# Every second quad's bf16 product and the softmax normalisation on GpSimd instead of VectorE

## The chip, the cores and the metric

The kernel runs on one core of a Trainium2 chip. The metric is the device time of one execution in microseconds (us), as the median of several runs. The engines of a core are TensorE (PE; PEld are its weight loads), VectorE (DVE), ScalarE (ACT), GpSimd (POOL) and the DMA queues, here issued from SyncE (SP).

## The reference, cut to what matters

A transformer block with adaptive layer norm: attention with 32 heads of width 20 over 2048 tokens, then a bilinear gated MLP without a nonlinearity.

```python
x = A_x                                        # (1, 2048, 640), bf16
mod = (silu(c) @ w_mod).reshape(1, 6, 1, -1)   # sa, ca, ga, sb, cb, gb
h = layernorm(x) * (1 + ca) + sa
q, k, v = split_heads(h @ wqkv)                # H = 32, Dh = 20
p = softmax(q @ k.T * Dh ** -0.5)              # 32 x 2048 x 2048 exponentials
x = x + ga * (merge_heads(p @ v) @ wo)
h = layernorm(x) * (1 + cb) + sb
x = x + gb * (((h @ w_gate) * (h @ w_up)) @ w_down)   # F = 1536
```

## The kernel before

**Tiling.** The queries are cut into five chunks (`CHUNKS`: 512, 512, 512, 256, 256 tokens). The heads form 8 sets of 4, one head in each 32-row stripe of TensorE. One chunk with one set of heads is an *item*; there are 40, taken in order. In an item the scores of 128 keys by 512 columns for one head are a *unit*.

**Exponentials in two ways.** Most units go to ScalarE: `fexp` (L1219) takes three or two PSUM banks at once, in turn from the sets 0 to 2 and 3 to 4, and writes the buffers `PP`. The others, four at a time (a *quad*, 93 in all, numbered by `qi`), get their exponential from integer arithmetic on VectorE:

- `fp1` (L1244), four times for each quad: one PSUM bank of scores plus a constant, as int16, to a slot of `DB` (two slots). The PSUM bank comes from `G`, banks 5 and 6, which the rounds of all projections and of the MLP use as well.
- `fm` (L1272): the low seven bits of `DB` become a bf16 mantissa factor in a slot of `DSS` (three slots).
- `fx` (L1277): the product of `DB`, read as bf16, with that slot, in place. It is the quad's first term, and it gives the `DB` slot back together with `fe`.
- `fe` (L1280): the exponent bits alone, into another slot of `DSS`: the quad's second term.

The PV matmuls (L1616) take ScalarE's `PP` and both terms of each quad, and add them up in PSUM bank 7, which holds one item at a time; column 0 of each head gathers the sum of the exponentials. When an item is complete, `item_end_tasks` (L1319) puts out four instructions in a chain: `t1` transposes bank 7 to `OT` (L1325), `t2` takes the reciprocals of the sums to `invT` (L1328), `t3` multiplies `OT` by them into `OTn` (L1330), and `t4` transposes this back to `OcT` (L1333), from where DMAs collect it in `Ocp` for the output projection. The chunk's MLP (`suffix`, L1366) is worked off while the next chunk's exponentials run; the last chunk's stands alone at the end. Its layer norm has two small steps on GpSimd, L1423 and L1425.

**The order is written by a planner.** `Sched` simulates the engines with a cost for each task, and takes for each engine at each moment the ready task of the lowest priority number; `emit_program` writes the orders found as five fixed instruction streams with semaphore waits. At run time each engine works through its own stream in that order, and an instruction that waits holds up all that stand behind it on its engine. The costs used for the parts concerned are `TS_4X, TT_2X = 600.0, 1145.0` (ns, for `fm`/`fe` and `fx`), 60 ns for a semaphore (`SEM`), and 60 ns of latency for a GpSimd task. The steps of a quad wait until bank 7 belongs to their item:

```python
t = Task("dve", dur, f, deps, prio=2.5 + .001 * qi, name=f"{name}.{qi}")
t.cond = lambda: it <= st_pv["item"]
```

How many quads an item has is a table (`QUADS`, L389), and the change leaves it as it is.

Of the kernel before, what the change touches and what calls it, by code (L numbers as in the profile page):

```python
# [6 lines left out]
ALU = mybir.AluOpType  # L7
# [58 lines left out]
class Slots:  # L66

    def __init__(self, ids, name=""):
        self.name = name
        self.free = [(i, []) for i in ids]  # L70
        self.hold = {}

    def avail(self, only=None):
# [9 lines left out]
        return best  # L83

    def take(self, k, refs=1):
        i, rel = self.free.pop(k)
        self.hold[i] = [refs, []]
        return i, rel

    def done(self, i, task):  # L90
        h = self.hold[i]
        h[0] -= 1
        h[1] = [x for x in h[1] if x.nbytes or x.eng != task.eng] + [task]
        if h[0] == 0:
            del self.hold[i]
            self.free.append((i, h[1]))

# [292 lines left out]
D_LEAD = 0.35  # L390
NB0, NSS = 2, 3
NPS = 4
TS_4X, TT_2X = 600.0, 1145.0
# [38 lines left out]
def build_kernel(nc, A_x, A_wqkv, A_wo, B_x, B_w_gate, B_w_up, B_w_down, c, w_mod, out):  # L432
    S, D, H, DH = A_x.shape[1], A_x.shape[2], 32, 20
    KD = D // 128
# [166 lines left out]

    G = Slots([5, 6], "G")
    GX = Slots([2, 3, 4], "GX")
    GC = Slots([0, 1], "GC")
# [142 lines left out]

    def quarters(n, lhs, rhs, st, sp):
        def one(x):
            return lambda e, b: e.matmul(ps[32 * x:32 * x + 32, b, 0:n], lhs()[:, 32 * x:32 * x + 32], rhs(),  # L750
                                         tile_position=(0, 32 * x), start=st, stop=sp, skip_group_check=True)
        return [one(x) for x in range(4)]
# [72 lines left out]
    def hT_rounds(tc, prio):  # L825
# [3 lines left out]
        for k in range(KD):  # L829
# [6 lines left out]
            def after(r, k=k):  # L836
# [6 lines left out]
            r = Round(mms, [t_xn[tc][i] for i in range(4)] + [p_id], after, prio, name=f"hT{tc}.{k}",  # L843
                      banks=GX if tc == 0 and k in (1, 3, 4) else None)
            t_hT[tc].append(r.evac[0])
# [212 lines left out]
    while ap < NA:  # L1058
        even = len(glist) % 2 == 0
        us = ubuf[ap:ap + (3 if even else 2)]  # L1060
        apos.append(ap)
        ap += len(us)
        glist.append((us, 0 if even else 3))
# [128 lines left out]
    act_tasks = []  # L1192
    gx_evac = [t_hT[0][k] for k in (1, 3, 4)]
    act_of = {}
# [56 lines left out]
    for qi, (it, us) in enumerate(dquads):  # L1251
# [30 lines left out]
        tm = term(fm, list(st_["p1"]), TS_4X, "M", slot=0)  # L1282
        term(fx, [tm], TT_2X, "X", src=0, last=True)
        term(fe, list(st_["p1"]), TS_4X, "EX", slot=1, src=1, last=True)
# [34 lines left out]
    def item_end_tasks(it):  # L1319
# [9 lines left out]
                                            OT[:, 0:n].rearrange("p (b c) -> p b c", c=32)[:, :, 0:1]), [t1], prio=1.5)  # L1329
        t3 = dve(sb_cost(n, 1.04), lambda e: e.tensor_tensor(  # L1330
            OTn[:, 0:n].rearrange("p (b c) -> p b c", c=32), OT[:, 0:n].rearrange("p (b c) -> p b c", c=32),
            invT[:, 0:nb32].unsqueeze(2).to_broadcast([128, nb32, 32]), ALU.mult), [t2], prio=1.5)
        t4 = dve(n * 1.1 + 65, lambda e: e.transpose(OcT[:, cell["s"], 0:n], OTn[:, 0:n]), [t3], prio=1.5)  # L1333
# [32 lines left out]
    def suffix(ci):  # L1366
# [88 lines left out]
        for fc in range(FT):  # L1455
            use_x = tail and fc < nsx
            wbuf, dm = [], []
            for w_, wv in enumerate((wgv, wuv)):
# [16 lines left out]
                dm.append(t)  # L1475
            gs = fc % 2
            for w_ in range(2):
                mms = []
# [202 lines left out]

    tail_added = [False]

    def d_wants():
# [78 lines left out]
    def pick_pe(t):  # L1763
        sc.pull("pe")
        g = pvstate["sidx"]
        if g < NG:
            ts, us = score_q[g]
            if acquire_ready(ts, t):
                start = mode_start("S", t)
# [33 lines left out]
        elif not tail_added[0]:  # L1803
            tail_added[0] = True
            la = [a for a in act_tasks[-2:]]
            if all(a.done is not None for a in la):
                for b in range(5):
                    G.add(b, la)
            else:
# [3 lines left out]
        if XFIRST and ring() >= XFIRST and pick_x(t):  # L1813
            just_s[0] = False
            return True
        cands = pv_candidates(t, PVCAP)
# [101 lines left out]
```

The softmax here doesn't subtract the row's maximum and nothing guards it: scores larger than these inputs give would overflow.

## Time and profile before

| | us |
|---|---|
| median of 3 runs (853.17 to 856.5) | 854.6 |
| the profiled execution | 851.11 |
| its span, from the first to the last instruction | 849.3 |
| busy: PE, DVE, ACT, POOL | 793.9, 719.6, 778.7, 30.6 |
| the 671 exponentials on ACT (L1220) | 763.0 |
| `fp1`, x372 | 250.4 |
| `fx`, x93 | 112.2 |
| `fm` and `fe`, x93 each | 63.3 each |
| `t3`, x40 | 23.1 |

Busy time counts an instruction from its start to its end, and two VectorE instructions in a row overlap by almost 0.1 us, so that VectorE's sum is a little above the time it was taken. The profile's groups give for each line of the kernel the engine, the tiles written and read, the count, the busy time and the mean of one, and the idle time ahead of them with the engine and line that ended it.

### The profile page before, as it was taken

How to read it: one execution, taken by the hardware profiler on the slowest of the kernel's cores; microseconds unless marked ns; L12 is line 12 of the kernel's file. 1: busy time of each engine (PE TensorE's matmuls, PEld its weight loads, DVE VectorE, ACT ScalarE, POOL GpSimd, SP SyncE). 2: the span in 40 equal slices, each digit the busy share in tenths (PEclk: the TensorE clock that was granted, in tenths of full speed). 3: DMA queues.
4: the chain of work that ended last, by engine and by line, in shares of the span. 5: the costliest groups of instructions: out<-in, count | busy, mean ns of one | idle time of the engine just before them, and what ended most of it. 6: DMA issues, size and time to landing. Idle time of an engine off the chain costs nothing.

```text
span 849.3 us, 28015 instructions
## 1 busy us (share of the span) xinstructions
PE 793.9 (93%) x12239; PEld 306.9 (36%) x12239; DVE 719.6 (85%) x1271; ACT 778.7 (92%) x700; POOL 30.6 (4%) x65
## 2 busy tenths in 40 slices
PE   8899999999998999999989999998999999999898
PEld 4432333322223222223323223232344443454477
DVE  7769988899999989898889999889789979677773
ACT  4568899999999999999999999999999999999931
POOL 2300000000001000000001000000011000000000
PEclk9989999999999999999999999999999999999999
DMA  9135222012240122310210122000300236115420
GB/s 296 37 97 158 61 68 58 7 44 76 75 124 18 33 60 57 109 57 13 68 40 6 24 65 56 14 12 14 70 33 6 59 76 135 38 46 113 105 59 20
DMA packets 114433, 53.19 MB, mean 63 GB/s; under 512 B 83359, under 2 KB 114311, under 8 KB 114311
## 3 DMA queue, kind: packets, MB, share of 16 engines
q1 hardware_dynamic: 113383, 50.25, 23.2%
q8 instruction: 97, 1.59, 0.8%
q10 hardware_dynamic: 928, 1.15, 0.4%
q14 instruction: 25, 0.20, 0.1%
HBM read 41.09 MB, written 7.99 MB: 58 GB/s over the span
## 4 chain that ended last, share of the span: by engine, by line
PE 38%; ACT 35%; DVE 16%; issue 11%; POOL 0%; ACTq 0%; DVEq 0%
ACT PP L1220 34%; PE ps_all L750 14%; PE ps_all L1186 11%; PE ps_all L1616 8%; DVE DB L1244 5%; DVE DSS L1277 2%; PE ps_all L917 1%; DVE st L805 1%; DVE DSS L1272 1%; DVE st L1420 1%; DVE xck L1410 1%; PE ps_all L832 1%; DVE wd L1174 1%; PE ps_all L1845 1%; DVE OT L1325 1%
## 5 line engine op out<-in xcount | busy, mean ns | idle before, releaser
L1220 ACT ACTIVATE PP<-ps_all 128x1536 bf16<-128x1536 f32 (+1 forms) x671 | 763.0, 1311 | 17.3 <-PE ps_all L1186 14.7
L1186 PE MATMUL ps_all<-QT,KT 32*128 32x512 bf16 (+1 forms) x2560 | 311.9, 342 | 32.1 <-ACT PP L1220 25.0
L1244 DVE TENSOR_SCALAR DB<-ps_all 128x512 int16<-128x512 f32 x372 | 250.4, 682 | 60.8 <-PE ps_all L1186 59.0
L1186 PEld LDWEIGHTS ps_all<-QT,KT 32*128 32x128 bf16 x2560 | 82.3, 91 | 269.8 <-ACT PP L1220 189.4
L1616 PE MATMUL ps_all<-PP,Vf 128*32 128x512 bf16 (+2 forms) x2112 | 166.3, 347 | 0.4 <-DVE OT L1325 0.2
L1277 DVE TENSOR_TENSOR DSS<-DB,DSS 128x2048 bf16<-128x2048 bf16 x93 | 112.2, 1207 | 0.0
L750 PE MATMUL ps_all<-h2T,stg 128*32 128x512 bf16 x1440 | 109.8, 382 | 1.2 <-DVE DB L1244 0.6
L1616 PEld LDWEIGHTS ps_all<-PP,Vf 128*32 128x32 bf16 (+1 forms) x2112 | 48.1, 94 | 87.9 <-issue 78.2
L1616 PE MATMUL ps_all<-DSS,Vf 128*32 128x512 bf16 (+2 forms) x896 | 75.5, 348 | 0.3 <-DVE DSS L1280 0.2
L1280 DVE TENSOR_SCALAR DSS<-DB 128x2048 int16<-128x2048 int16 x93 | 63.3, 681 | 2.1 <-PE ps_all L1616 2.1
L1272 DVE TENSOR_SCALAR DSS<-DB 128x2048 int16<-128x2048 int16 x93 | 63.3, 681 | 1.6
L750 PE MATMUL ps_all<-wd,hprod 128*32 128x320 bf16 x1152 | 56.2, 302 | 1.2 <-DVE DB L1244 0.7
L750 PEld LDWEIGHTS ps_all<-h2T,stg 128*32 128x32 bf16 x1440 | 33.2, 95 | 37.4 <-issue 15.4
L750 PE MATMUL ps_all<-wo,Ocp 128*32 128x320 bf16 x640 | 34.1, 301 | 1.5 <-DVE DB L1244 1.1
L750 PEld LDWEIGHTS ps_all<-wd,hprod 128*32 128x32 bf16 x1152 | 27.1, 96 | 20.6 <-issue 10.2
L1485 DVE CAST gsb<-ps_all 128x512 bf16<-128x512 f32 (+1 forms) x48 | 29.5, 614 | 3.9 <-PE ps_all L750 3.7
L1325 DVE STREAM_TRANSPOSE OT<-ps_all 128x512 f32<-128x512 f32 (+1 forms) x40 | 24.2, 605 | 10.1 <-PE ps_all L1616 9.8
L917 PE MATMUL ps_all<-hT,wq 128*32 128x512 bf16 x375 | 29.8, 395 | 2.1 <-DVE DB L1244 0.9
L1423 POOL TENSOR_SCALAR sd<-mv 128x1 f32<-128x1 f32 x14 | 6.3, 446 | 707.0 <-DVE mv L1422 707.0
L1616 PEld LDWEIGHTS ps_all<-DSS,Vf 128*32 128x32 bf16 (+1 forms) x896 | 24.5, 96 | 19.2 <-issue 8.0
L750 PE MATMUL ps_all<-wV,hT 128*32 128x320 bf16 x640 | 29.9, 312 | 0.9 <-ACT hT L838 0.3
L1496 DVE TENSOR_TENSOR hprod<-ps_all,gsb 128x512 bf16<-128x512 f32 x36 | 24.6, 683 | 5.4 <-PE ps_all L750 5.1
(108 smaller groups left out, 518.8 us busy)
## 6 DMA issues: line engine op xcount, KB each, us to landing
stg<-in_B_w_gate_dram SPq DMA_DIRECT2D x50, 160.0 KB, 2.5
stg<-in_B_w_up_dram SPq DMA_DIRECT2D x50, 160.0 KB
QT<-q_rows SPq DMA_DIRECT2D x22, 128.0 KB, 2.4
wm<-in_w_mod_dram SPq DMA_DIRECT2D x3, 800.0 KB
x<-in_A_x_dram SPq DMA_DIRECT2D x7, 320.0 KB
KT<-k_rows SPq DMA_DIRECT2D x64, 32.0 KB, 1.9
xck<-in_A_x_dram SPq DMA_DIRECT2D x3, 640.0 KB, 4.2
wd<-in_B_w_down_dram SPq DMA_DIRECT2D x1, 1920.0 KB
```

The lines of the kernel that those rows point to most:

```text
L750: return lambda e, b: e.matmul(ps[32 * x:32 * x + 32, b, 0:n], lhs()[:, 32 * x:32 * x + 32], rhs(), tile_position=(0, 32 * x), start=st, s ...
L917: f = [lambda e, b_, k=k, x=x: e.matmul(ps[x:x + min(32, w - x), b_, :], wx[:, k, r0 + x:r0 + min(x + 32, w)], hT[tc][:, k, :], tile_posit ...
L1186: ems.append(lambda e, i=i, kt=kt: e.matmul(dstf()[:, i * u.n:(i + 1) * u.n], KT[32 * u.s:32 * u.s + 32, u.j, kt * 128:(kt + 1) * 128], QT ...
L1220: return e.activation(PPs[g % 2][:, cellp["p"], 0:nu * 512], ps[:, b0:b0 + nu, :].rearrange("p b c -> p (b c)"), AFT.Exp, scale=ESCALE)
L1244: return e.tensor_scalar(DB0[:, st_["slot"], x * 512:(x + 1) * 512], bank(cell["b"]), EBIAS, 0.0, op0=ALU.add, op1=ALU.max)
L1272: return e.tensor_scalar(DSS[:, st_["ss"][0], :], DB0[:, st_["slot"], :], 0x7F, 0x3F00, op0=ALU.bitwise_and, op1=ALU.bitwise_or)
L1277: return e.tensor_tensor(d, DB0[:, st_["slot"], :].bitcast(BF16), d, ALU.mult)
L1280: return e.tensor_scalar(DSS[:, st_["ss"][1], :], DB0[:, st_["slot"], :], 0x7F80, 2, op0=ALU.bitwise_and, op1=ALU.bitwise_or)
L1325: t1 = Task("dve", n * 1.1 + 70, lambda e: e.transpose(OT[:, 0:n], ps[:, BPV, 0:n]), [], prio=0.0, name=f"T1.{it}")
L1485: f = lambda e: e.tensor_copy(gsb[:, gs, 0:n], ps[:, r.b["b"], 0:n])
L1496: f = lambda e: e.tensor_tensor(hprod[:, fc, 0:n], ps[:, r.b["b"], 0:n], gsb[:, gs, 0:n], ALU.mult)
L1616: ems.append(lambda e, i=i, kt=kt, stt=stt, stp=stp: e.matmul(ps[32 * s:32 * s + mc, BPV, 0:u.n], Vf[:, (kt * H + 4 * u.j + s) * VW:(kt * ...
```

## The change

Of every second quad (`qi` even, 47 of 93) the product leaves VectorE: it becomes four GpSimd instructions of 512 columns each, every one of them waiting for the one before. For the other 46 quads `fx` stays. `t3` of every item but the last (39 of 40) becomes one GpSimd instruction. The planner gets 2.2 ns for each column and 150 ns for each such instruction (200 ns for `t3`), so that all five streams are planned anew. The arithmetic is the same.

```diff
+HEADG = 0
+X_POOL, X_PIECES, POOL_NS = 2, 4, 2.2
+GU_ONE = 0
+XCONT = 0
+T3_POOL = 1
+HEAD_OUT = 2
...
         tm = term(fm, list(st_["p1"]), TS_4X, "M", slot=0)
-        term(fx, [tm], TT_2X, "X", src=0, last=True)
+        if X_POOL and qi % X_POOL == 0:
+            deps = [tm]
+            for x in range(X_PIECES):
+                w = 2048 // X_PIECES
+
+                def fxp(e, x=x, w=w, st_=st_):
+                    d = DSS[:, st_["ss"][0], x * w:x * w + w].bitcast(BF16)
+                    return e.tensor_tensor(d, DB0[:, st_["slot"], x * w:x * w + w].bitcast(BF16), d, ALU.mult)
+                t = Task("pool", w * POOL_NS + 150.0, fxp, deps, prio=.1 * qi, name=f"XP.{qi}")
+
+                def on_p(task, x=x, st_=st_):
+                    if x == X_PIECES - 1:
+                        sB0.done(st_["slot"], task)
+                        st_["src"][0] = [task]
+                t.on_start = on_p
+                sc.add(t)
+                deps = [t]
+        else:
+            term(fx, [tm], TT_2X, "X", src=0, last=True)
         term(fe, list(st_["p1"]), TS_4X, "EX", slot=1, src=1, last=True)
...
-        t3 = dve(sb_cost(n, 1.04), lambda e: e.tensor_tensor(
+        f3 = lambda e: e.tensor_tensor(
             OTn[:, 0:n].rearrange("p (b c) -> p b c", c=32), OT[:, 0:n].rearrange("p (b c) -> p b c", c=32),
-            invT[:, 0:nb32].unsqueeze(2).to_broadcast([128, nb32, 32]), ALU.mult), [t2], prio=1.5)
+            invT[:, 0:nb32].unsqueeze(2).to_broadcast([128, nb32, 32]), ALU.mult)
+        if T3_POOL and it < len(items) - 1:
+            t3 = pool(n * 2.2 + 200, f3, [t2], prio=0)
+        else:
+            t3 = dve(sb_cost(n, 1.04), f3, [t2], prio=1.5)
```

The remaining lines of the diff (`retire`, `HEADG`, `GU_ONE`, `XCONT`) add branches that the constants above leave out of use.

## The prediction

> **What bounds the kernel now.** I read the page's busy line first, then the busy time by stretches, then the waits, then the line of each operation concerned.
>
> The busy line names two candidates for the bound:
>
> ```profile
> PE 793.9 (93%) x12239; PEld 306.9 (36%) x12239; DVE 719.6 (85%) x1271; ACT 778.7 (92%) x700; POOL 30.6 (4%) x65
> ```
>
> The stretches (columns: length, then busy us and count of PE, PEld, DVE, ACT, POOL) decide between them:
>
> ```profile
> 60.00:100.00 40.00, 37.69 (x483) 13.34 (x474) 36.10 (x62) 32.75 (x29) 0.00 (x0) 0.94 0.36 102
> ...
> 300.00:400.00 100.00, 96.67 (x1194) 28.96 (x1190) 90.08 (x143) 99.50 (x89) 0.00 (x0) 0.98 0.23 61
> ...
> 825.00:849.00 24.00, 20.66 (x692) 17.91 (x680) 7.88 (x18) 4.47 (x12) 0.00 (x0) 1.00 0.08 25
> ```
>
> From 100 to 800 us the seven stretches give ACT 695.1 of 700: ScalarE's exponentials set the time, and 4.9 us is all that could be won there. The last exponential ends at 814; the 35 us after it are the last chunk's MLP on PE, which the change doesn't touch. VectorE has the load of a full engine, but not the last word, as the waits show (who waited for whom: us in total, times, longest us):
>
> ```profile
> PEld ps_all L1186 <- ACT PP L1220: 189.4, 470, 1.2
> ...
> DVE DB L1244 <- PE ps_all L1186: 59.0, 83, 2.7
> ...
> PE ps_all L1186 <- ACT PP L1220: 25.0, 69, 1.0
> PEld ps_all L1186 <- DVE DB L1244: 24.4, 64, 0.8
> ...
> PEld ps_all L750 <- DVE DB L1244: 19.4, 49, 0.8
> ...
> ACT PP L1220 <- PE ps_all L1186: 14.7, 17, 2.8
> ```
>
> The reader is to see three things. TensorE stands before scores for ACT 470 + 69 = 539 times, 214.4 / 539 = 0.40 us each: this is its slack. VectorE waits 59 us for scores, so it has room already. And PE waits for `fp1` to empty a bank of `G` over a hundred times: VectorE's punctuality matters more than its load.
>
> [...] On POOL, the 128x1 steps of the layer norm:
>
> ```profile
> 253.23 0.57 POOL L1425 TENSOR_TENSOR rs<-sd,mhalf 128x1 f32<-128x1 f32 x1
> ...
> 271.52 1.11 POOL L1423 TENSOR_SCALAR sd<-mv 128x1 f32<-128x1 f32 x1 [6.13 <-DVE mv L1422]
> ...
> 633.67 1.61 POOL L1425 TENSOR_TENSOR rs<-sd,mhalf 128x1 f32<-128x1 f32 x1
> ```
>
> L1423 takes 0.22 at its median and 1.11 here, L1425 0.57 or 1.61. On VectorE at those moments:
>
> ```profile
> 271.35 0.64 DVE L1280 TENSOR_SCALAR DSS<-DB 128x2048 int16<-128x2048 int16 x1
> 271.90 0.69 DVE L1272 TENSOR_SCALAR DSS<-DB 128x2048 int16<-128x2048 int16 x1
> ...
> 633.64 1.22 DVE L1277 TENSOR_TENSOR DSS<-DB,DSS 128x2048 bf16<-128x2048 bf16 x1
> ```
>
> GpSimd ended 0.04 us after `fm` and 0.42 after `fx`. VectorE held up by GpSimd isn't seen: no `fm`, `fe` or `fx` lasts over 0.70 or 1.23, but nothing on GpSimd lasts long enough to try it. [...]
>
> **The change part by part.** The durations are of the profiled execution (851.11 us, span 849.3); the median of the runs lies 3.5 us above it, and I carry the sum over to it.
>
> 1. *VectorE loses* 47 products at 1207 ns, 56.7 us, and 39 of the 40 `t3`, 23.1 less the one of 0.4 that stays, 22.7 us. Together 79 of 719.6 us, 11%. Where ACT is at 99% this is worth nothing by itself. It can be worth something from the first `fm` at 56 to 100 us, where ACT lost 8.0 us in six waits for PE (0.36, 0.16, 2.13, 1.16, 1.84, 2.39), and VectorE runs almost without a gap from 75 to 94 us. There the products of quads 0, 2, 4 and two `t3` go: 3 x 1.13 + 2 x 0.60 = 4.6 us (start to start). Between 0 and 8.0 us; I take a third of what is freed, **-1.5**.
>
> 2. *GpSimd gains* 188 pieces and 39 `t3`. No such operation is in the trace. [...] an estimate of 1.12 us a piece. From below, the 128x512 memset's 0.53 (L1116, one write, no read); from above 1.5, if bf16 or the hand-over costs more. GpSimd then reads for 188 x 1.12 = 211 us, and for 35 us in `t3` (24 of 512 columns, 15 of 256): 246 of the 758 us between 56 and 814, 32%. It has the time.
>
> 3. *The new lock on VectorE.* 93 `fm`, 93 `fe`, 46 `fx` and some 30 others (weights times gate, `xn`) can meet a piece: 262 x 0.32 = 84 meetings, half a piece each, 47 us. So VectorE keeps perhaps 32 of the 79 us, less than nothing if each meeting costs a whole piece (94). Behind the waiting instruction stand `fp1` and the evacuations, for which PE waits, and behind PE's wait stand the next scores. PE waits for `fp1` 172 times in 372 (adding up its list of waits), so half of the lateness gets to PE. What absorbs it there: the 0.40 above, and the other set of banks, where an exponential lasts 763.0 / 671 = 1.14 on average and scores take some 0.5, so 0.6 more. Half a piece ends inside this 1.0 us; a whole piece, or `fm` and `fe` both late, does not. One meeting in five at 0.3 us is **+5**. Bounds: 0 (VectorE always passes) and 84 x 0.56 x 0.46 = 22.
>
> 4. *The first term comes later.* `fe` follows `fm` on VectorE at once[...]; then four pieces, 0.09 apart (L1423 to L1425: 252.92 + 0.22 to 253.23), 4.8; another meeting now and then, 0.3. That is 5.7 us after `fm`, where `fx` took 1.2. The order is built on 4 x (1276 + 60 + 60) = 5.6 us, so PE's matmuls on `DSS` are placed for it. Now such a wait is small (L1616 for `DSS`: 5.6 us in 21 waits). Late by 0.1 is nothing; a further 1.04 (L1425's stretch) in some quads passes the 1.0 us by a little: **+2** in all, between 0 and 45 (next part). The later release of `DB` (two slots) is covered: a quad fills its slot in 6 us (`fp1` from 303.36 to 309.45), now holds it some 7 more, and the slot is wanted again after 16 (two quads of 760 / 93). If that cover fails, `fp1` starts later, and the lead of 0.35 item (8 us) that units have in `D_LEAD` pays. `DSS` has three slots for about 19 us of holding in each 16.
>
> 5. *`t3` and the small steps.* `t1` to `t4` took 5.0 us (308.17 to 313.16); with a piece ahead of `t3`, and 1.12 for 0.68, 6.7, and `OT` is wanted again after 12 us at the earliest. SP's DMAs from `OcT` start that much later, far ahead of the output projection that needs them. L1423 and L1425 stand behind a piece, and VectorE's `xn` behind them: 14 times at most half a piece. Taken at nothing; with the cover gone, the 7 us of VectorE lie in step 3's margin.
>
> Sum: -1.5 + 5 + 2 = +5.5, so 856.6 for the profiled execution and **860** for the median.
>
> **The rivals.** *A, PE waits for GpSimd (much slower).* If a piece takes 1.5, or every piece meets a lock, the term is late by 2 us in each of 47 quads, scores stand behind the waiting PV matmul, and past 1.0 us each quad takes 0.9 from ACT: 47 x 0.9 = 42, 897. It decides from a chain 1 us over the planned 5.6. For it: the stretches of 1.04 above. Against: the four pieces leave gaps, and `fe` can be over before they begin. *B, all hidden:* PE's 0.40 us and the banks absorb every meeting, the ramp gains as much as is lost: 854.6 (851 to 858). For it: ACT waited 4.2 us in 700, although PE waited for VectorE over a hundred times. Against: those waits were planned, the meetings are not. *C, faster:* between 56 and 100 us VectorE is what keeps PE from the scores. With 4.6 us freed there and the six waits going by three quarters, 6 us: 848.6. It decides if `fp1` and the evacuations in that stretch start at least 0.5 us sooner each. Against: the waits of 2.39 and 2.13 come after projection matmuls of PE (L750, L917 in the chain that ended last), which keep their length.
>
> **How the numbers follow.** A measurement here tells about 0.5% from no change: 850.3 to 858.9. My forecast (857 to 867) 0.38, of which 0.10 falls below 858.9; A (867 to 900) 0.19; B, or a change that doesn't do what it says, 0.27; C 0.16. So faster 0.16, same 0.37, slower 0.47. The range leaves out the lower end of C and the upper half of A: 847 to 886; the forecast's own is 857 to 867.
>
> **What would show it.** Right: POOL near 300 us busy, pieces 1.1 to 1.3 from start to start; DVE near 640 plus gaps ahead of `fm`, `fe` and `fx`; ACT still over 98% from 100 to 800, with its waits for PE at some 10 us, not 4.2. Rival A is seen in PE's waits for `DSS` written by POOL, dozens over 1 us. Rival C is seen in ACT's busy time from 56 to 100. I am wrong if ACT's idle time in the middle grows by 20 us, or if GpSimd's pieces stretch VectorE's `fm` and `fe` not at all.

## The result and the profile after

| us | before | after |
|---|---|---|
| median of the runs | 854.28 | 881.69 |
| range of the runs | 853.17 to 856.5 | 881.43 to 883.3 |
| profiled execution | 851.11 | 881.72 |
| its span | 849.3 | 879.9 |

The kernel became slower: the ratio is 1.032, with a 95% interval of 1.0297 to 1.0346. That is 27 us where the forecast had 5.5. It went the way that was forecast, by five times the amount. The traced executions lie 30.6 us apart, since the one before is 3 us below its median.

The busy line of the page, after:

```profile
PE 817.3 (93%) x12272; PEld 313.0 (36%) x12272; DVE 682.7 (78%) x1185; ACT 784.6 (89%) x700; POOL 308.0 (35%) x292
```

VectorE lost the load that it was to lose and GpSimd took it on, yet ScalarE's share fell from 92 to 89%. The stretches (length, then busy us and count of PE, PEld, DVE, ACT, POOL, then the granted clock of PE) say where:

```profile
60.00:100.00 40.00, 35.10 (x438) 11.73 (x430) 32.56 (x52) 33.45 (x29) 16.18 (x12) 0.91 0.36 98
100.00:200.00 100.00, 94.74 (x1211) 30.06 (x1209) 78.47 (x124) 91.55 (x81) 33.80 (x27) 0.97 0.17 44
200.00:300.00 100.00, 94.36 (x1063) 28.31 (x1061) 84.19 (x139) 93.73 (x82) 43.01 (x40) 0.93 0.25 65
300.00:400.00 100.00, 96.64 (x1194) 29.43 (x1186) 83.64 (x133) 99.19 (x88) 36.54 (x29) 1.00 0.25 65
...
841.00:880.00 39.00, 32.45 (x934) 26.72 (x923) 16.50 (x42) 4.53 (x13) 3.45 (x4) 0.96 0.06 20
```

Up to 100 us nothing changed for ScalarE (65.7 us busy against 65.1). From 100 to 800 its seven stretches add up to 673.5 of 700, where they were 695.1. The stretch from 300 to 400 is still full; in the two ahead of it ScalarE is idle for 8.5 and 6.3 us, and in the four after it for about 3 each. The last exponential ends at 841 and no longer at 814, which is the whole difference of the two traces but for 3.5 us in the MLP behind it.

The groups of the page (count, busy us, mean ns of one, then idle us ahead of them and what ended it), first the exponentials before, then the groups after:

```profile
L1220 ACT ACTIVATE PP<-ps_all 128x1536 bf16<-128x1536 f32 (+1 forms) x671 | 763.0, 1311 | 17.3 <-PE ps_all L1186 14.7
```

```profile
L1239 ACT ACTIVATE PP<-ps_all 128x1536 bf16<-128x1536 f32 (+1 forms) x671 | 769.1, 1271 | 39.2 <-PE ps_all L1205 27.1
...
L1309 POOL TENSOR_TENSOR DSS<-DB,DSS 128x512 bf16<-128x512 bf16 x188 | 235.8, 1254 | 271.7 <-DVE DSS L1291 261.4
...
L1299 DVE TENSOR_SCALAR DSS<-DB 128x2048 int16<-128x2048 int16 x93 | 79.1, 851 | 0.6 <-PE ps_all L1685 0.6
...
L1291 DVE TENSOR_SCALAR DSS<-DB 128x2048 int16<-128x2048 int16 x93 | 70.0, 753 | 1.7
```

(`fe` is now L1299, `fm` L1291, `fp1` L1263, scores L1205, PV L1685; GpSimd's pieces are L1309.) The idle time ahead of the exponentials grew from 17.3 us to 39.2, and their own busy time by 6.1: taken one by one, the 671 last 880 us in sum before and 853 after (671 x the mean), of which 117 us and 84 are overlap of one with the next. `fm` and `fe` have the work they had, but 70.0 and 79.1 us instead of 63.3 each: VectorE is held up beside GpSimd's pieces, the direction that the trace before could not show. (*Lock* is a name for this and no more: an instruction lasts longer while one of the other engine runs. What makes it last longer is not shown.) It is seen at one place in the timeline (start, duration):

```profile
311.21 0.68 DVE L1291 TENSOR_SCALAR DSS<-DB 128x2048 int16<-128x2048 int16 x1
...
311.97 2.71 POOL L1309 TENSOR_TENSOR DSS<-DB,DSS 128x512 bf16<-128x512 bf16 x2 [5.07 <-DVE DSS L1291]
...
312.41 1.26 DVE L1299 TENSOR_SCALAR DSS<-DB 128x2048 int16<-128x2048 int16 x1
```

`fe` comes 0.44 us after the first piece and lasts 1.26 us, not 0.68. Who waited for whom, in the whole execution (us in total, times, longest us):

```profile
PEld ps_all L1205 <- ACT PP L1239: 152.8, 398, 1.1
DVE DB L1263 <- PE ps_all L1205: 95.5, 133, 2.4
...
ACT PP L1239 <- PE ps_all L1205: 27.1, 38, 2.8
PEld ps_all L1205 <- DVE DB L1263: 27.0, 74, 1.1
PEld ps_all L769 <- DVE DB L1263: 24.2, 52, 1.2
...
ACT PP L1239 <- PE ps_all L1685: 10.0, 8, 2.3
...
PEld ps_all L1685 <- DVE DSS L1299: 5.3, 17, 0.7
```

Three things are to be seen. TensorE's weight loads for scores stand before ScalarE 398 times, not 470. TensorE waits for `fp1` more. And ScalarE has a wait that was small before: for PV (L1685), 10.0 us in 8 where there were 2.1 in 2. An exponential needs a free `PP` buffer, and a PV matmul frees it. No wait of TensorE for a term written by GpSimd is in the whole list.

### The profile page after: what moved, and what is told of

The parts are those of the page before. It is cut to its first block, busy times and chain, and to the rows that moved or that the text cites. A ratio compares the mean times of both kernels' runs of the same rounds, so it can differ in the third digit from the quotient of the medians.

```text
span 879.9 us, 28227 instructions
## 1 busy us (share of the span) xinstructions
PE 817.3 (93%) x12272; PEld 313.0 (36%) x12272; DVE 682.7 (78%) x1185; ACT 784.6 (89%) x700; POOL 308.0 (35%) x292
## 3 DMA queue, kind: packets, MB, share of 16 engines
q1 hardware_dynamic: 113383, 50.25, 22.7%
q10 hardware_dynamic: 928, 1.15, 0.4%
## 4 chain that ended last, share of the span: by engine, by line
PE 49%; DVE 26%; ACT 15%; issue 6%; POOL 1%; DMA 1%; POOLq 0%; ACTq 0%; DVEq 0%
PE ps_all L1205 16%; PE ps_all L769 16%; ACT PP L1239 15%; PE ps_all L1685 11%; DVE DB L1263 9%; PE ps_all L936 3%; DVE DSS L1291 3%; DVE DSS L1299 2%; PE ps_all L884 2%; DVE OT L1362 1%; DVE DSS L1296 1%; DVE st L824 1%; DVE st L1461 1%; PE ps_all L1923 1%; DMA wm<-in_w_mod_dram 1%
## 5 line engine op out<-in xcount | busy, mean ns | idle before, releaser
L1239 ACT ACTIVATE PP<-ps_all 128x1536 bf16<-128x1536 f32 (+1 forms) x671 | 769.1, 1271 | 39.2 <-PE ps_all L1205 27.1
L1205 PE MATMUL ps_all<-QT,KT 32*128 32x512 bf16 (+1 forms) x2560 | 317.4, 345 | 23.9 <-ACT PP L1239 11.8
L1309 POOL TENSOR_TENSOR DSS<-DB,DSS 128x512 bf16<-128x512 bf16 x188 | 235.8, 1254 | 271.7 <-DVE DSS L1291 261.4
L1263 DVE TENSOR_SCALAR DB<-ps_all 128x512 int16<-128x512 f32 x372 | 251.1, 683 | 96.3 <-PE ps_all L1205 95.5
L1205 PEld LDWEIGHTS ps_all<-QT,KT 32*128 32x128 bf16 x2560 | 83.3, 91 | 261.2 <-ACT PP L1239 152.8
L1685 PE MATMUL ps_all<-PP,Vf 128*32 128x512 bf16 (+2 forms) x2112 | 166.5, 349 | 1.7 <-DVE OT L1362 1.5
L1367 POOL TENSOR_TENSOR OTn<-OT,invT 128x512 bf16<-128x512 f32 (+1 forms) x39 | 44.9, 1151 | 205.8 <-DVE invT L1365 205.8
L1685 PEld LDWEIGHTS ps_all<-PP,Vf 128*32 128x32 bf16 (+1 forms) x2112 | 47.7, 95 | 90.4 <-issue 80.4
L1299 DVE TENSOR_SCALAR DSS<-DB 128x2048 int16<-128x2048 int16 x93 | 79.1, 851 | 0.6 <-PE ps_all L1685 0.6
L1685 PE MATMUL ps_all<-DSS,Vf 128*32 128x512 bf16 (+3 forms) x896 | 76.3, 352 | 0.8 <-DVE DSS L1299 0.7
L1291 DVE TENSOR_SCALAR DSS<-DB 128x2048 int16<-128x2048 int16 x93 | 70.0, 753 | 1.7
L1296 DVE TENSOR_TENSOR DSS<-DB,DSS 128x2048 bf16<-128x2048 bf16 x46 | 56.8, 1235 | 0.0
L1554 DVE CAST gsb<-ps_all 128x512 bf16<-128x512 f32 (+1 forms) x48 | 29.5, 614 | 11.5 <-PE ps_all L769 11.4
L1923 PE MATMUL ps_all<-ident 128*128 128x512 bf16 x84 | 30.5, 422 | 5.6 <-DVE DB L1263 1.9
L936 PE MATMUL ps_all<-hT,wq 128*32 128x512 bf16 x375 | 32.6, 422 | 2.1 <-DVE DB L1263 0.9
L1362 DVE STREAM_TRANSPOSE OT<-ps_all 128x512 f32<-128x512 f32 (+1 forms) x40 | 24.2, 604 | 11.7 <-PE ps_all L1685 11.7
```

The lines of the kernel that those rows point to most:

```text
L936: f = [lambda e, b_, k=k, x=x: e.matmul(ps[x:x + min(32, w - x), b_, :], wx[:, k, r0 + x:r0 + min(x + 32, w)], hT[tc][:, k, :], tile_posit ...
L1205: ems.append(lambda e, i=i, kt=kt: e.matmul(dstf()[:, i * u.n:(i + 1) * u.n], KT[32 * u.s:32 * u.s + 32, u.j, kt * 128:(kt + 1) * 128], QT ...
L1239: return e.activation(PPs[g % 2][:, cellp["p"], 0:nu * 512], ps[:, b0:b0 + nu, :].rearrange("p b c -> p (b c)"), AFT.Exp, scale=ESCALE)
L1263: return e.tensor_scalar(DB0[:, st_["slot"], x * 512:(x + 1) * 512], bank(cell["b"]), EBIAS, 0.0, op0=ALU.add, op1=ALU.max)
L1291: return e.tensor_scalar(DSS[:, st_["ss"][0], :], DB0[:, st_["slot"], :], 0x7F, 0x3F00, op0=ALU.bitwise_and, op1=ALU.bitwise_or)
L1296: return e.tensor_tensor(d, DB0[:, st_["slot"], :].bitcast(BF16), d, ALU.mult)
```

## The experiments

All ratios are to the kernel before, with 95% intervals; "kernel after" is the 1.032 above. The base was 853.5, 853.2, 852.9, 853.1 and 852.7 us in the five groups of runs. "ScalarE's waits" are those between 100 and 790 us, from the profiled execution: before, 4.2 us for scores in 9 waits and 0.2 us for PV in one; after, 16.4 in 28 and 7.6 in 7.

Two theories stood against each other: the *lock* (GpSimd's pieces hold up VectorE, with the order blameless), and the *order* (the planner's new streams are worse, whatever GpSimd does). Rival A, a first term that is late at run time, was the third.

### The two halves of the change

`x_only`: the product moved, `t3` left on VectorE.

```diff
-T3_POOL = 1
+T3_POOL = 0
```

> The products of every second quad on GpSimd, t3 back on VectorE. Theory 'lock' ([...] fm, fe and fx on VectorE stretch, fp1 behind them comes late, TensorE and then ScalarE wait): nearly all of the loss stays, ratio 1.02 to 1.035, with fm and fe together at about 20 us over the 126.6 of before. Theory 't3' (the chain at each item's end, held up by a piece ahead of it on GpSimd, delays the PV matmuls of the next item): the ratio falls to 1.01 or less. Theory 'order' (the streams as planned anew are worse by themselves): can go either way, since this is planned anew too.

Measured: 887.65 us, 1.041 [1.038, 1.044]. It is slower than the whole change, and above every ratio that was named for it but a new order's. `t3_only`: the reverse.

```diff
-X_POOL, X_PIECES, POOL_NS = 2, 4, 2.2
+X_POOL, X_PIECES, POOL_NS = 0, 4, 2.2
```

> Only the multiply by the reciprocals on GpSimd, all products on VectorE. Theory 'lock': 39 instructions of 1.15 us hold VectorE for at most a few us, so the ratio is 1.00 to 1.006. Theory 't3': a good part of the loss, 1.01 to 1.02.

Measured: 864.59 us, 1.013 [1.008, 1.018]; `fe` takes 68.5 us there. Each half is slower, and the halves don't add up, so that something other than the two instructions' own cost plays along. Every one of these kernels has its own order of the streams.

### The order without the lock

`order_only`: the streams of the kernel after, instruction for instruction, but each piece multiplies 2 columns instead of 512.

```diff
-d = DSS[:, st_["ss"][0], x * w:x * w + w].bitcast(BF16)
-return e.tensor_tensor(d, DB0[:, st_["slot"], x * w:x * w + w].bitcast(BF16), d, ALU.mult)
+d = DSS[:, st_["ss"][0], x * w:x * w + 2].bitcast(BF16)
+return e.tensor_tensor(d, DB0[:, st_["slot"], x * w:x * w + 2].bitcast(BF16), d, ALU.mult)
```

> The changed kernel with its five streams, semaphores and planned costs as they are, but each GpSimd piece multiplies 2 columns instead of 512; the rest of the product is left out. t3 stays whole. [...] Theory 'lock' and theory 'late term': ratio 1.000 to 1.010, fm and fe back at 0.68 us each. Theory 'order': 1.025 to 1.035, as the whole change, though fm and fe are back at 0.68.

Measured: 868.29 us, 1.018 [1.015, 1.021]. With the pieces all but gone, 15 us of the 27 stay, and 12 to 13 go: as the streams are the same, these are the price of the pieces' length. `t3` stays whole on GpSimd here, so that a little of the lock remains in the 15 us: `fm` and `fe` take 130.2 us together, against 126.6 before and 149.1 after.

```profile
L1299 DVE TENSOR_SCALAR DSS<-DB 128x2048 int16<-128x2048 int16 x93 | 66.1, 711 | 1.9 <-PE ps_all L1685 1.9
L1291 DVE TENSOR_SCALAR DSS<-DB 128x2048 int16<-128x2048 int16 x93 | 64.1, 689 | 1.7
```

ScalarE's waits in it:

```profile
ACT PP L1239 <- PE ps_all L1205: 9.3, 18, 1.4
ACT PP L1239 <- PE ps_all L1685: 7.0, 7, 1.6
```

The seven waits for PV are those of the kernel after, at the same places; they belong to its order. They are about half of what ScalarE loses in it: its busy time from 100 to 800 us is 12.5 us less than before. `late_nolock`: the same streams, with each piece replaced by two 128x1 steps that take 0.62 us each. The four pieces then take 4.95 us at their median, after 5.23, so that the term is nearly as late, but VectorE is not held (`fm` and `fe` 130.2 us, as with 2 columns).

```diff
...
-    return e.tensor_tensor(d, DB0[:, st_["slot"], x * w:x * w + w].bitcast(BF16), d, ALU.mult)
-t = Task("pool", w * POOL_NS + 150.0, fxp, deps, prio=.1 * qi, name=f"XP.{qi}")
+    return e.tensor_tensor(scr[:, 0:1], mone[:, 0:1], mhalf[:, 0:1], ALU.pow)
+def fxq(e):
+    return e.tensor_tensor(scr[:, 1:2], mone[:, 0:1], mhalf[:, 0:1], ALU.pow)
+t = Task("pool", w * POOL_NS + 150.0, [fxp, fxq], deps + [p_mh], prio=.1 * qi, name=f"XP.{qi}")
```

> The changed kernel, but each GpSimd piece is two powers of one column on scratch data, some 0.57 us each, instead of 512 products; the product is left out. The first term comes as late as in the changed kernel[...]. Theory 'lock': as with 2 columns, 1.000 to 1.012, fm and fe at 0.68. Theory 'late term' (TensorE waits for GpSimd's last piece): 1.025 to 1.035, with TensorE's waits for the scratch steps of GpSimd in the trace.

Measured: 866.32 us, 1.016 [1.012, 1.021], the waits for PV again 7.0 us in 7. So a term that comes late at run time costs nothing over `order_only`: rival A falls for this kernel. What is left is the order in which the planner put things, and `t3`'s hold.

### How much does any new order cost?

Three kernels that change no instruction, only a planner's cost. `null_a` and `null_b` are the kernel before; `after_null` is the kernel after.

```diff
# null_a
-TS_4X, TT_2X = 600.0, 1145.0
+TS_4X, TT_2X = 600.0, 1155.0
# null_b
-TS_4X, TT_2X = 600.0, 1145.0
+TS_4X, TT_2X = 595.0, 1145.0
# after_null
-t = Task("pool", w * POOL_NS + 150.0, fxp, deps, prio=.1 * qi, name=f"XP.{qi}")
+t = Task("pool", w * POOL_NS + 165.0, fxp, deps, prio=.1 * qi, name=f"XP.{qi}")
```

> The kernel before, no instruction moved or changed; only the planner is told 1155 ns instead of 1145 for fx, which is enough for it to write other orders. Theory 'chance' (the order of before is a lucky one among many that the planner writes, and any change of a cost loses it): ratio 1.005 to 1.02, with ScalarE's idle time from 100 to 800 us at 10 to 20 us. Theory 'structure' (the order of the change is worse because its first term comes 4 us later): 1.000 within 0.005, idle time near the 4.9 us of before.

> The kernel before with 595 ns instead of 600 as the planned cost of fm and fe, nothing moved. 'Chance': 1.005 to 1.02 here too, and not the same as for 1155 ns. 'Structure': 1.000 within 0.005.

> The changed kernel, every instruction as it is, but the planner adds 165 ns instead of 150 to a GpSimd piece, so that other orders are written. 'Chance' with the lock added: 1.02 to 1.045, not the same as 1.032. 'Structure': 1.032 within 0.005.

Measured: `null_a` 861.5, 1.010 [1.006, 1.013]; `null_b` 855.31, 1.003 [1.001, 1.005]; `after_null` 883.72, 1.036 [1.033, 1.040]. `null_a` is the uncomfortable one: 10 ns more in a cost, and it has waits for PV too:

```profile
ACT PP L1220 <- PE ps_all L1616: 6.9, 5, 3.4
ACT PP L1220 <- PE ps_all L1186: 6.7, 8, 1.6
```

An order drawn anew can therefore cost 1% by chance alone, and differences of that size between kernels with streams of their own decide nothing. `order_b` asks whether the order's loss comes back in a second draw: the streams of `after_null`, with 2 columns in a piece.

```diff
-    d = DSS[:, st_["ss"][0], x * w:x * w + w].bitcast(BF16)
+    d = DSS[:, st_["ss"][0], x * w:x * w + 2].bitcast(BF16)
...
-t = Task("pool", w * POOL_NS + 150.0, fxp, deps, prio=.1 * qi, name=f"XP.{qi}")
+t = Task("pool", w * POOL_NS + 165.0, fxp, deps, prio=.1 * qi, name=f"XP.{qi}")
```

> 2 columns in each piece, in the orders planned with 165 ns (the changed kernel in these orders: 1.036). Theory 'lock': the difference to 1.036 is again 0.012 to 0.016, so 1.020 to 1.024. If the lock's price depends on the order by chance: anything from 1.01 to 1.036.

Measured: 869.2 us, 1.019 [1.015, 1.023]; waits for PV 7.5 us in 7. The loss comes back with the same size. But this is not a second draw in full: VectorE's stream is the one of `order_only` for its first 425 instructions of 1185, up to 284 us in that trace, and four of the seven waits for PV, 3.8 of the 7.0 us, lie there in both, from 171 to 182 us in `order_only` and from 167 to 178 us here. `late_plan` is the kernel before with the lateness in the plan alone: the planner is told that every second `fx` has 4.4 us of latency.

```diff
-term(fx, [tm], TT_2X, "X", src=0, last=True)
+term(fx, [tm], TT_2X, "X", src=0, last=True).lat = 4440.0 if qi % 2 == 0 else DVE_LAT
```

> The kernel before with no instruction moved: all products stay on VectorE, but the planner is told that the product of every second quad is there 4.4 us later than it is, so that TensorE's matmuls on it and the free slot of DB are planned as late as in the change. Theory 'structure' (the later term by itself makes the order worse): near 1.018. Theory 'chance': within 1.002 and 1.012, as the two orders planned with other costs.

Measured: 874.64 us, 1.027 [1.023, 1.032], but the four runs are 864, 873, 876 and 878; without the slowest the median is 872.8, 1.023. The traced one is the fastest, 1.3% above the kernel before, with 8.8 us of waits for PV in 4, the longest 3.5. GpSimd does nothing in it that it didn't do before. So a plan that reckons with a late first term can lose by itself, and this one lost more than the two plans with 10 and 5 ns changed; but it is one draw.

### Which quads bring the loss

If the late term hurts because it holds bank 7 (an item's PV sum is complete only with its last term, and the next item's PV matmuls must wait for the bank), then the last quad of an item is what matters. Both of these use pieces of 2 columns and leave `t3` on VectorE. `order_last` moves the last quad of each item alone (39 quads), `order_notlast` only quads that are not the last (50, in the first three chunks).

```diff
-        if X_POOL and qi % X_POOL == 0:
+        if us is item_info[it]["quads"][-1]:                                  # order_last
+        if items[it][0] < 3 and us is not item_info[it]["quads"][-1]:         # order_notlast
```

> 2 columns in each GpSimd piece (the rest of these products is left out)[...]; t3 on VectorE; the quads moved are the last one of each item, 39 of 93. Theory 'item end' (a late last term holds bank 7, PV falls behind, the PP buffers stay full): 1.012 to 1.025, with 5 us or more of ScalarE's waits for the PV matmuls from 100 to 800 us. Theory 'chance': between 1.002 and 1.012, these waits as likely small as large.

> 2 columns in each piece, t3 on VectorE; the quads moved are all but the last of each item in the first three chunks, 50 of 93, more than in the change. Theory 'item end': 0.998 to 1.008, with ScalarE's waits for the PV matmuls from 100 to 800 us at 2 us or less. Theory 'any later term' (slots of DB and DSS held longer): 1.012 to 1.025 here as well.

Measured: `order_last` 860.6, 1.009 [1.007, 1.011]; `order_notlast` 850.7, 0.997 [0.995, 0.999]. Their waits from 100 to 790 us, `order_last` first:

```profile
ACT PP L1239 <- PE ps_all L1205: 5.7, 7, 1.2
ACT PP L1239 <- PE ps_all L1685: 4.3, 4, 2.8
```

```profile
ACT PP L1239 <- PE ps_all L1205: 0.9, 3, 0.5
ACT PP L1239 <- PE ps_all L1685: 0.2, 1, 0.2
```

Moving 50 quads without the last ones has, in this stretch, no more waits for PV than before, and ScalarE is busy for 698.7 of 700 us between 100 and 800. (Ahead of 100 us one such wait lasts 6.7 us.) Moving 39 last ones has four. That fits the theory of the item's end, but doesn't show it. The 1.009 of `order_last` lies below the range that this theory gave and inside the one for chance, and `null_a` has more waits for PV with nothing moved. `order_notlast` also leaves the last two chunks alone, where three of the seven waits of `order_only` lie. And the other four, from 171 to 182 us, are in neither `order_last` nor `order_notlast`, while `null_a` has four with 6.2 us from 162 to 175. So the order costs what it costs; why it does stays open.

`order_notlast` also prices the aim of the change: with 50 products off VectorE and next to nothing on GpSimd, the gain is 0.3%. Even this may be TensorE's clock, as the next part shows.

### The lock in orders that lose nothing

`notlast_full`: the streams of `order_notlast`, with all 512 columns in each piece.

```diff
-        if X_POOL and qi % X_POOL == 0:
+        if items[it][0] < 3 and us is not item_info[it]["quads"][-1]:
```

> The orders of order_notlast (0.997 with 2 columns in a piece) with all 512 columns in each piece, so that nothing is left out: the product of 50 quads, never the last of an item, on GpSimd. Theory 'lock and item end are two separate parts': the lock's price of 0.011 to 0.017 comes on top, 1.008 to 1.014, with ScalarE's waits for PV still under 1 us and fm and fe together near 143 us. Theory 'the lock only hurts where PV is late already': 0.997 to 1.003.

Measured: 877.0 us, 1.029 [1.024, 1.035]. Between two kernels with one and the same order, the length of the pieces makes 3.2%, some 27 us, about twice what the theory of two separate parts had for it (0.011 to 0.017). Its waits, and a piece of its timeline:

```profile
ACT PP L1239 <- PE ps_all L1205: 20.4, 28, 3.0
ACT PP L1239 <- PE ps_all L1685: 0.2, 1, 0.2
```

```profile
383.08 5.23 POOL L1309 TENSOR_TENSOR DSS<-DB,DSS 128x512 bf16<-128x512 bf16 x4 [2.30 <-DVE DSS L1291]
...
383.51 5.14 DVE L1193 TENSOR_TENSOR wd<-wd,gab 128x640 bf16<-128x640 bf16 x4
...
388.58 0.68 DVE L1263 TENSOR_SCALAR DB<-ps_all 128x512 int16<-128x512 f32 x1
...
389.31 0.61 PE L1923 MATMUL ps_all<-ident 128*128 128x512 bf16 x1 [3.60 <-DVE DB L1263]
...
390.50 1.02 ACT L1239 ACTIVATE PP<-ps_all 128x1024 bf16<-128x1024 f32 x1 [2.98 <-PE ps_all L1205]
```

This is the whole chain on five lines. VectorE has four small products of weights and gate, 0.48 us each in `order_notlast`, to do while GpSimd works off its four pieces. It gets in once per piece (1.43 us for one of them at the median), and the four take 5.14 us. Behind them stands `fp1`, which is not drawn out itself (0.68 us) but begins 5.07 us after the first of them, where it is 1.61 us in `order_notlast`. PE has waited 3.60 us for the bank when it comes (0.00 us busy from 385.9 to 389.3), and ScalarE 2.98 us for the scores. What each meeting costs adds up here, where they follow each other. This is seen at one place, and the kernel after doesn't have it: there these products keep their 0.48 us.

The granted clock joins in here. The shortest of the stretches at half clock in the trace before lasts 3.41 us (one of them from 382.46 to 385.87: clock 0.50 in it, 1.00 in the 3.41 us on either side). In windows of that length ahead of, and in, two stretches at half clock of `notlast_full` (columns as above; the number after POOL's is the clock):

```profile
345.99:349.40 3.41, 2.15 (x26) 0.53 (x22) 3.41 (x5) 3.35 (x4) 2.88 (x2) 1.00 0.34 83
349.40:359.60 10.20, 10.20 (x79) 1.85 (x73) 4.90 (x8) 6.36 (x5) 4.58 (x5) 0.50 0.17 39
383.59:387.00 3.41, 1.89 (x17) 0.49 (x13) 3.41 (x4) 3.41 (x4) 3.20 (x3) 0.99 0.00 0
387.00:397.20 10.20, 7.89 (x43) 1.59 (x43) 8.47 (x16) 5.40 (x5) 1.28 (x1) 0.50 0.01 2
```

and a window as long in `order_notlast`, from the same product of weights and gate on:

```profile
365.65:369.06 3.41, 3.03 (x26) 0.88 (x22) 3.41 (x9) 3.41 (x4) 0.75 (x2) 1.00 0.07 19
```

PE was busy for only 2.15 and 1.89 of 3.41 us, and then ran at half clock for 10.2 us, in which ScalarE was busy for 6.36 and 5.40. After 95 us and up to the last exponentials PE spends 13.7 us at half clock before, 30.7 after, 0 in `order_notlast` (its trace is of one of its fastest runs, 847.4 us against 850.7) and 27.3 in `notlast_full`. At these two places the slow clock follows upon a window in which PE had little to do. Not at every one, if PE's busy time by the trace is the measure: in `notlast_full` the drop at 663.4 us follows 2.9 us of work in 3.4, and before the one at 382.5 follows 3.2, while 2.0 from 219.7 to 223.1 us in `notlast_full` brought none. What sets the clock is not shown.

How much of the 27 us is the slow clock was not tried apart, but the runs allow an estimate. Among the runs of one kernel the slower ones have the lower mean clock: by 4.6 us for each 0.01 in 96 runs of the kernel before, by about 5 in `order_notlast` and in `notlast_full`. The mean is 0.969 in `notlast_full` and 0.987 in `order_notlast`, so that some 9 of the 27 us go with the clock; for the kernel after against `order_only` (0.971 and 0.977) it is some 2.5 of 12, and for `late_plan` (0.964) some 7 of its 22. The kernel before has 0.979, and by the same estimate the 0.3% gained by `order_notlast` is no more than the clock. Which of the two, waiting or slow clock, brings on the other, these runs don't tell. Of the 20.4 us of waits for scores in `notlast_full`, 11.7 lie in such stretches or just behind them. That GpSimd's work can cost time without the slow clock is seen further down: the traces of `pieces8` and `pieces8_2` have none of it between 95 us and the last exponential, and are 13 us apart.

`notlast_fe` lets `fe` go ahead of `fm`, so that it is over before the pieces begin.

```diff
-t = Task("dve", dur, f, deps, prio=2.5 + .001 * qi, name=f"{name}.{qi}")
+t = Task("dve", dur, f, deps, prio=2.5 + .001 * qi - (.0005 if name == "EX" else 0), name=f"{name}.{qi}")
```

> As notlast_full, but fe is planned ahead of fm for all quads, so that it stands before GpSimd's first piece and not behind it. Planned anew, so chance adds up to 0.01. If fe behind fm carries the lock's price: fm and fe together under 135 us and a ratio of 0.998 to 1.008. If the price comes from every meeting alike: fm and fe together still over 140 us and a ratio of 1.008 to 1.02.

Measured: 878.36 us, 1.029 [1.026, 1.033]; `fe` takes 72.1 us where it took 79.1, but `fm` 73.4 where it took 66.3. The meeting was moved to the other instruction, not taken away.

### The length of one hold

These keep the streams of the kernel after (`pieces8` and `pieces8_2` have their own) and change how long GpSimd works in one go. `half_cols` multiplies 256 of the 512 columns; `split_256` all 512 in two instructions back to back; `two_1024` 1024 columns in the first and third piece and a tiny step in the second and fourth.

```diff
# half_cols
...
-    d = DSS[:, st_["ss"][0], x * w:x * w + w].bitcast(BF16)
+    d = DSS[:, st_["ss"][0], x * w:x * w + w // 2].bitcast(BF16)
# split_256, once with h = 0 and once with h = 1
...
+    c = x * w + h * (w // 2)
+    d = DSS[:, st_["ss"][0], c:c + w // 2].bitcast(BF16)
# two_1024
...
+    c, m = (x // 2 * 1024, 1024) if x % 2 == 0 else (x // 2 * 1024, 0)
+    if m == 0:
+        return e.tensor_tensor(sd[:, 0:1], mhalf[:, 0:1], mhalf[:, 1:2], ALU.mult)
+    d = DSS[:, st_["ss"][0], c:c + m].bitcast(BF16)
```

> The changed kernel in its own order, but each GpSimd piece multiplies 256 columns instead of 512, and the other half of the product is left out[...]. Theory 'lock' (the part of the loss beyond the new order, 1.032 against 1.018 with 2 columns[...]): about halfway, 1.021 to 1.028, with fm and fe together at some 137 us between 130.2 and 149.1. If the loss needs a whole piece, as the prediction's 1.0 us of slack has it: near 1.018.

> The changed kernel in its own order, every product made, but each piece of 512 columns is two GpSimd instructions of 256, one behind the other without a wait between them. [...] Theory 'lock with a threshold' (only a hold of some 1.1 us gets through the slack of TensorE): near 1.018, with fe at 0.77 on average as with half of the columns[...].

> The changed kernel in its own order, every product made, but the first and third piece take 1024 columns each, and the second and fourth are a tiny step on scratch data. [...] Theory 'lock with a threshold': clearly more than 1.032, 1.045 to 1.08, since a hold far beyond 1.0 us goes through to ScalarE, with fe at 1.1 or more on average. Theory 'lock by total time': 1.032 as before.

`pieces8` plans eight pieces of 256 columns, each waiting for the one before; `pieces8_2` has its streams with 2 columns.

```diff
-X_POOL, X_PIECES, POOL_NS = 2, 4, 2.2
+X_POOL, X_PIECES, POOL_NS = 2, 8, 2.2
...
-t = Task("pool", w * POOL_NS + 150.0, fxp, deps, prio=.1 * qi, name=f"XP.{qi}")
+t = Task("pool", w * POOL_NS + 90.0, fxp, deps, prio=.1 * qi, name=f"XP.{qi}")
```

> The change with eight pieces of 256 columns instead of four of 512, each waiting for the one before, planned anew; t3 on GpSimd. Theory 'a wait lets VectorE in': against the same orders with 2 columns only 0.000 to 0.006 more, with fe at 0.77 or less on average. [...]

> The orders of the eight pieces, with 2 columns in each and the rest of these products left out: what the order alone costs there. From 1.008 to 1.025 (the last terms of items come even later than with four pieces).

Measured, each beside the kernel with the same streams and 2 columns:

| kernel | us | ratio | same streams, 2 columns | points lost to the length | VectorE longer, us |
|---|---|---|---|---|---|
| `half_cols` | 868.49 | 1.018 [1.015, 1.021] | 1.018 | 0 | 7 |
| `pieces8` | 872.19 | 1.022 [1.017, 1.027] | 1.011 [1.007, 1.014] | 1.1 | 12 |
| `split_256` | 882.12 | 1.035 [1.032, 1.038] | 1.018 | 1.7 | 16 |
| kernel after | 881.69 | 1.032 [1.030, 1.035] | 1.018 | 1.4 | 22 |
| `notlast_full` | 877.0 | 1.029 [1.024, 1.035] | 0.997 | 3.2 | 29 |
| `two_1024` | 907.89 | 1.066 [1.062, 1.070] | 1.018 | 4.8 | 42 |

The last column is what `fm`, `fe`, `fx` and the small products take beyond the kernel with 2 columns, with `t3` in `notlast_full`. (`pieces8_2` itself took 860.04 us.) With `half_cols` the lock is there, 7 us of it, and it costs nothing. In the others, each microsecond by which VectorE's instructions are drawn out goes with 0.5 to 1.0 us of time (12 us for 22 in the kernel after, 41 for 42 in `two_1024`). In the three kernels with one and the same order a like number of instructions is held (41 in `half_cols`, 49 after, 43 in `two_1024`, of which `t3` has its share, for `order_only` has 11), by 0.3, 0.55 and 1.05 us each on average, and the price goes 0, 12, 41 us: what counts in these three is for how long an instruction is held, and the holds of 0.3 us vanish. It is not GpSimd's total that counts: the pieces of `two_1024` take 209 us, those of the kernel after 236, and `two_1024` loses over three times as much. Its `fe`:

```profile
L1299 DVE TENSOR_SCALAR DSS<-DB 128x2048 int16<-128x2048 int16 x93 | 101.2, 1089 | 0.2 <-PE ps_all L1688 0.2
```

Shorter instructions back to back (`split_256`) bring nothing, but for a second reason too: there the four pieces' work takes longer, and PE's waits for a term of GpSimd, which the kernel after doesn't show, come to 17 us:

```profile
L1310 POOL TENSOR_TENSOR DSS<-DB,DSS 128x256 bf16<-128x256 bf16 x376 | 275.8, 754 | 254.4 <-DVE DSS L1291 244.2
L1687 PE MATMUL ps_all<-DSS,Vf 128*32 128x512 bf16 (+3 forms) x896 | 75.8, 353 | 5.9 <-POOL DSS L1310 5.0
...
L1687 PEld LDWEIGHTS ps_all<-DSS,Vf 128*32 128x32 bf16 (+1 forms) x896 | 22.9, 96 | 27.9 <-POOL DSS L1310 12.3
```

So here is rival A after all, in a kernel whose chain of eight lasts longer than the plan has it. `pieces8` has such waits too, 11.5 us in 18, so that the points of these two are not the lock's alone, and whether a wait between short pieces lets VectorE in stays undecided: up to 0.6 points were forecast if it does and 1.2 or more if it doesn't, and 1.1 lie between.

## Why the prediction was right and wrong

**What bounds the kernel: right.** ScalarE's exponentials set the time, the relief of VectorE was worth next to nothing by itself (`order_notlast`: 0.3%), and the loss came as idle time of ScalarE in the middle.

**Step 1, the work taken off: right in size, wrong by a little in the ramp.** 55.4 and 22.7 us left VectorE's groups, 78 against 79. That the busy line has 682.7 and not the 640 named as a mark comes mostly from what step 3 put back, 28 us. The rest, some 14 us, is overlap: the busy line counts time in which two instructions overlap once, and is not the sum of their durations, which went from 795.5 to 744.8 us. The -1.5 us for the ramp did not come: ScalarE was busy 65.7 us up to 100 against 65.1, and the stretch from 60 to 100 gained 0.7. Rival C falls with it.

**Step 2, GpSimd's price: right.** A piece takes 1.155 us at its median and 1.254 on average; four in a row take 5.23 us, 1.235 from start to start (medians), inside the 1.1 to 1.3 foreseen; POOL is busy 308 us (near 300 foreseen). The 1.12 foreseen was the author's estimate (512 columns at the planner's 2.2 ns); the trace before had no such operation.

**Step 3, the lock: right in kind, its passing on mis-sized.** Foreseen were 84 meetings and 47 us of lateness on VectorE, of which one meeting in five gets through at 0.3 us: +5, or 0.06 us for each meeting. That VectorE would be held, and which of its instructions, was the author's assumption; the trace before showed only GpSimd held up. Measured: fewer meetings and less lateness, 49 held instructions among `fm`, `fe`, `fx` and the layer norm's steps, and 28 us against before (`fe` 15.8, `fm` 6.7, the layer norm's steps 3.9, `fx` 1.3, `wo` 0.8), and yet the lock of the pieces costs 12 us in the orders of the kernel after (1.032 against 1.018 for `order_only`), 0.25 us for each, and 27 in those of `order_notlast`. The lateness of one meeting was sized right (half a piece, 0.56 us foreseen, 0.55 measured). The term that failed is the share that gets through the slack of 1.0 us. Slack there is, for `half_cols` costs nothing, but holds of 0.55 us on average were to end inside it, all but one in five, and don't. That meetings add up when they follow each other, as at 383 us of `notlast_full`, where `fp1` comes 3.5 us late behind four pieces, is one way past it; whether it is the one in the kernel after is not shown. The direction of the lock that the trace before had left open, VectorE held by GpSimd, is seen now: `fe` goes up to 1.65 us and `fm` to 1.69, where neither lasted over 0.70, and `fp1` keeps its 0.68 (0.69 at most). It shows as longer instructions, and not as the gaps ahead of `fm`, `fe` and `fx` that were named as a mark.

**Step 4, the later first term: the step that failed most.** It was costed at +2, and the order as a whole costs 15 us (`order_only`, with `t3`'s hold in it). The reckoning compared the chain at run time with the plan (5.7 against 5.6 us), and that part held: from `fm` to the end of the fourth piece it takes 5.3 us at the median, over 5.6 in 11 of 47 quads. The 5.7 had 0.6 us in it for `fe` ahead of the pieces, the author's estimate, and where the first piece begins just behind the start of `fe` (18 of the 47 quads, as at 166.02 and 166.19 us), it lasts 1.53 us at the median where the first pieces of the other quads last 1.15. `late_nolock` costs nothing beyond the order, no wait of PE for GpSimd's term is in the lists of the kernel after, and rival A fell. What was put at nothing without a reason is the plan itself: a plan with a term 4.4 us later is another plan, with other streams. With the lateness planned but nothing moved, one draw lost 2.3 to 2.7% (`late_plan`). The cover named was `DB`, `DSS` and the lead of the units; the `PP` buffers, for which ScalarE waits 7.0 us in `order_only` and 0.2 before, were not named.

Why the new order is worse stays open. How much of the 15 us is chance in the planner's draw does too: 10 ns in one cost brought 1.010 with 6.9 us of waits for PV, and the two draws of the change itself that agree (1.018 and 1.019) have their first 284 us in common.

**Step 5, `t3` and the small steps at nothing: wrong in part.** The kernel with `t3` alone on GpSimd is 1.3% slower. `t3` takes 1.14 us there on average and meets VectorE too: `fe` grows to 68.5 us and `fm` to 64.3, from 63.3 each. What of the 1.3% is the lock and what the new order, which by chance alone can cost 1.0%, was not tried apart.

**The sum.** -1.5 + 5 + 2 stands against 0 + 12 + 15, with what `t3` costs inside the 15. That 881.69 lies in the outer range (847 to 886) is luck: the range reached so far up for rival A, whose mechanism is not what happened, and the result is 15 us beyond the forecast's own 857 to 867. One mark named for "wrong" came true: ScalarE's idle time in the middle grew by 21.6 us, past the 20 that were set, and its waits for PE there came to 24 us, not to some 10.

What stays open besides: why the lock alone costs twice as much in an order without the PV loss (27 us against 12; some 18 against 10 without the clock's part as estimated).

## What to carry to other kernels

Before work is moved to GpSimd, set the length of one of its instructions against the slack behind VectorE's: here holds of 0.3 us vanished, holds of 0.55 and 1.05 did not. Look also for instructions of VectorE that follow each other beside a run of GpSimd's: at 383 us of `notlast_full` four of 0.48 us took 5.14, and ScalarE then waited 2.98. Where a planner writes the order, a longer latency is a new order; run it with the moved work shrunk to two columns, which prices the order apart from the length of the work. Run several null changes beside it to see what a new draw alone does, and before explaining a difference of 1% look at the granted clock of the runs: 0.01 of its mean went with 4.6 us of 853 here.

## What the runs showed of the hardware

- GpSimd's product of two bf16 inputs takes 0.272, 0.764, 1.254 and 2.227 us on average for 2, 256, 512 and 1024 columns (`order_only`, `half_cols`, the kernel after, `two_1024`): some 1.9 ns for each column and about 0.28 us besides, with what VectorE's instructions add to it.
- VectorE's instruction that is held appears in the profile as a longer instruction, not as a gap ahead of it: `fm` at 0.69 us and at 1.69, with 1.7 us of idle time ahead of all 93 where it was 1.6 before; `wd` at 0.48 and, in `notlast_full`, at 1.43.
- While GpSimd works off four pieces, each with a semaphore wait in between, VectorE gets in once per piece (5.14 us for four `wd` products beside 5.23 for four pieces, at one place in `notlast_full`).
- In the traced executions the same order of instructions ran without half-clock stretches of PE between 95 us and the last exponential, and with 27.3 us of them when GpSimd's pieces went from 2 columns to 512.
- Among 96 runs of the kernel before, 0.01 less of the mean granted clock goes with 4.6 us more, of some 853.
